# Four attention layers on one core: the second chunk's q moved to another buffer, under a new order of the steps

## The chip, the core and the metric

The kernel runs on one core of a Trainium2 chip. A core has five engines that each take their instructions strictly in the order in which they were issued: TensorE (PE in the profile, its weight loads PEld), VectorE (DVE), ScalarE (ACT), GpSimd (POOL) and SyncE (SP), which here issues nearly all DMAs. The engines wait for each other and for DMAs by semaphores. Operands lie in SBUF (128 partitions); TensorE writes to PSUM, which has eight banks here.

The metric is the time of one execution on the device in microseconds, as the median of several.

## What is computed

The input x has 2048 positions of 512 values. Four layers follow each other, A, B, A, B, each of the form x + attention(layernorm(x)), all in 32-bit floats. Both kinds have 32 heads of 16 values; they differ in what a position sees.

```python
# A: eight positions, two apart, backwards
idx = pos[:, None] - (arange(8) * 2)[None, :]
logits = einsum("bhsd,bhswd->bhsw", q, kg) * scale   # kg, vg: k, v gathered at idx
o = einsum("bhsw,bhswd->bhsd", softmax(logits), vg)
return o @ wo
# B: the last 256 positions
mask = (i - j >= 0) & (i - j < 256)
p = softmax(where(mask, q @ k.T * scale, -1e9))
return (p @ v) @ wo
x = x + A(layernorm(x)); x = x + B(layernorm(x)); x = x + A(layernorm(x)); x = x + B(layernorm(x))
```

## The kernel before

**Tiling.** The 2048 positions are cut into eight chunks of 256. The plan names the chunks of the first pair of layers A0 to A7 and B0 to B7 and those of the second pair A8 to A15 and B8 to B15. A chunk of B needs the chunk of A before it and k and v of its predecessor, so the chunks of the two layers run interleaved: A0, then B0 beside A1, B1 beside A2, and so on. Ahead of all stand "pA" and "pB", the loading and splitting of the weights.

**Precision.** Each float operand of a projection is split into a high and a low 16-bit part; a product is three matmuls, high by high, high by low and low by high. A projection step in the plan is such a triple: lines 1015 to 1017 for q, k and the transposed form, 1035 to 1038 for v and the output.

**A chunk of layer A** (`layer_a`, from line 1100). x is loaded (1088) and normalized (`norm`: means and squares on ScalarE, 936 and 939, a power on GpSimd, 942 to 948, the normalized tile `xn` on ScalarE, 964). Its high part is a copy (974), its low part a difference (970), and four transposing DMAs (976 and 977, on SP) bring both parts of both halves into `xh` and `xl`, with the features on the partitions. Chunk A0 and all chunks of B transpose on TensorE instead (986, 990, 995, 996). There are two buffers for `xn` and two for each of `xh` and `xl`. Then come sixteen steps each for q, k and v; ScalarE copies them out of PSUM (1131 for q, 1133 for k and v). Products of q with the shifted k (1152, sixteen tiles of 128x512 in four groups, on DVE or GpSimd) are summed over a head's values by TensorE (1160, one instruction group for each four tiles, so four sums). The softmax over eight logits is a chain on DVE (1183, 1186, the exponential on ScalarE 1212, 1189, 1192, 1195) with a high part (a copy on ScalarE, 1216) and a low part (1203, on DVE or GpSimd). TensorE spreads the weights over the heads' rows (1229), DVE multiplies by v (1242, eight times), GpSimd or DVE adds over the eight positions (1249 to 1251, or 1247), and `finish` splits the result (1059, 1061), projects it and adds it to x (1069).

**A chunk of layer B** (`layer_b`). After the projections, high and low parts of k and q (1273 on ScalarE, 1276 on DVE) go through DRAM (SP, 1286) into stacked operands `stk` (SP, 1297). A first pass of scores (1339, 1342) serves only the row maxima (DVE; 1352 in the first chunk of a layer, 1360 and 1356 later), which join the stack as two more rows through DRAM (1375 to 1399). A second pass (1432, 1434) gives scores less their maxima, ScalarE takes the exponential into a probability tile (1438), GpSimd masks it (1447), TensorE multiplies by v (1464), and ScalarE evicts (1500).

**Buffers that the change touches.** `po4` holds one q buffer (tag `q`) and one each for the outputs of A and B. `pp6` has three buffers of 6 KB a partition (tag `p6`): they stage the output weights of A and B at the start and hold B's probability tiles `p` later. For chunk A1 alone, k and v lie in buffers of another pool (`pos`) and its output in B's output buffer, so that A2 can use the `pkv` pair.

**What sets the order.** Each step is added to a plan with the engine it runs on, what it reads and writes, and a place number from a table written out in the file, `ORDER`, with one list for each chunk. An engine takes its steps by place. A negative number means that the step runs on its second choice of engine, at place -1 less the number; steps with two choices have an `alt`. A planner's model then merges the five queues into one order of issue and hands out the PSUM banks; it does not change the order within an engine. A list `W` places 110 triples of idle matmuls ("IDLE", line 1579), which compute nothing.

In the list of A2, entries 22 to 37 are the places of the q steps on TensorE, and after two for ScalarE's copies come the sixteen of the k steps. Entries 13, 14, 18 and 19 are its transposing DMAs on SP.

Of the kernel before, what the change touches and what calls it, by code (L numbers as in the profile page):

```python
# [11 lines left out]
F32 = mybir.dt.float32  # L12
# [6 lines left out]
P = 128  # L19
S = 2048  # L20
# [3 lines left out]
C = 256  # L24
NCH = S // C
W = 8
# [652 lines left out]
def kernel(  # L679
# [20 lines left out]
    def buf(name, shape, dtype, tag, label, cap=None, group=0):  # L700
        p, n = pools[name]
        return Buf(p, cap or n, shape, dtype, tag, label, group)
# [916 lines left out]
```

## Time and profile before

| | |
|---|---|
| median of three executions | 1426.83 us (1426.66 to 1429.48) |
| profiled execution | 1428.45 us, of which span 1426.7 us |
| mean granted TensorE clock | 0.957 |
| busy: PE, DVE, ACT, POOL | 1340.1, 1127.4, 817.5, 689.6 us |
| DMA | 130.46 MB, mean 91 GB/s |

The span runs from the first to the last instruction of the program. Busy time is what an engine spent on instructions, without waits. The granted clock is the share of full speed that the throttle gave TensorE. In the order in time of one engine, a line shows the start and the duration in us, the engine, the line of the kernel, the operation, what it writes and reads, how many are merged in it, and in brackets how long the engine stood idle before and what ended that. In a table of stages each engine has its busy time and, in brackets, its instructions. In a line of a group the numbers are the busy time in us, the mean of one in ns, and the idle time before them.

### The profile page before, as it was taken

The page shows a single profiled execution, that of the slowest core. Times are in us where ns is not written, and L with a number is a line of the kernel's source. Part 1 is how long each engine was busy: PE and PEld are TensorE (multiplying, and loading weights), DVE is VectorE, ACT ScalarE, POOL GpSimd, SP SyncE. Part 2 cuts the span into 40 slices and gives each one's busy share as a digit, 9 for nine tenths or more (in the row PEclk, how much of TensorE's full clock was granted, in tenths as well). Part 3 has the DMA queues.
Part 4 walks back from the last instruction along what each step waited for, and adds up shares of the span by engine and source line. Part 5 has one row for each costly group of instructions (what it writes and reads, how often), then busy time and mean ns, then how long its engine had stood idle before and what let it go on. Part 6 is the DMA issues. An engine that isn't in the chain of part 4 may idle for free.

```text
span 1426.7 us, 35354 instructions
## 1 busy us (share of the span) xinstructions
PE 1340.1 (94%) x13918; PEld 788.4 (55%) x13918; DVE 1127.4 (79%) x2095; ACT 817.5 (57%) x1296; POOL 689.6 (48%) x829
## 2 busy tenths in 40 slices
PE   9986989999899999989999898998999999999998
PEld 7741646546365564746556374654637456474654
DVE  6878696896978879697986859689696968869694
ACT  7732545565585556556565454656567555646664
POOL 4434353472835427362562716366273644727333
PEclk9986999999999999999999998999999999999999
DMA  8233242333242333424234143322333233242231
GB/s 248 78 72 85 73 100 71 93 85 99 70 122 68 72 100 97 114 54 116 66 97 122 45 115 90 111 69 72 107 86 114 69 91 88 82 118 65 79 100 54
DMA packets 135944, 130.46 MB, mean 91 GB/s; under 512 B 68448, under 2 KB 94560, under 8 KB 135776
## 3 DMA queue, kind: packets, MB, share of 16 engines
q1 hardware_dynamic: 135520, 127.93, 33.1%
q8 instruction: 109, 1.79, 0.5%
q14 instruction: 59, 0.48, 0.1%
q10 hardware_dynamic: 256, 0.26, 0.1%
HBM read 67.11 MB, written 43.48 MB: 78 GB/s over the span
## 4 chain that ended last, share of the span: by engine, by line
PE 64%; DVE 13%; POOL 7%; ACT 5%; issue 5%; DMA 4%; SPq 3%; ACTq 0%; POOLq 0%; DVEq 0%
PE banks L1015 10%; PE banks L1016 8%; PE banks L1017 8%; PE banks L1464 8%; PE banks L1037 4%; PE banks L1035 4%; PE banks L1432 4%; PE banks L1038 4%; PE banks L1160 4%; DVE pw L1242 3%; PE banks L1339 3%; DVE m L1356 3%; ACT p L1438 2%; POOL pw L1249 2%; PE banks L1342 2%
## 5 line engine op out<-in xcount | busy, mean ns | idle before, releaser
L1438 ACT ACTIVATE p<-banks,sclB 128x768 f32<-128x768 f32 x480 | 417.6, 899 | 241.5 <-PE banks L1434 194.8
L1447 POOL TENSOR_SCALAR_AFFINE_SELECT p<-p 128x1024 f32<-128x1024 f32 x240 | 262.4, 1101 | 334.6 <-ACT p L1438 325.2
L1356 DVE TENSOR_REDUCE m<-banks 128x2 f32<-128x512 f32 x448 | 297.6, 687 | 4.1
L1360 DVE COPY_PREDICATED banks<-maskt,banks 128x256 f32<-128x256 int16 x448 | 179.0, 424 | 80.8 <-PE banks L1342 79.6
L1464 PE MATMUL banks<-p,v 128*32 128x128 f32 (+1 forms) x3840 | 196.0, 332 | 5.3 <-POOL p L1447 4.3
L1152 DVE TENSOR_TENSOR pr<-kv,q 128x512 f32<-128x512 f32 x225 | 152.8, 731 | 37.2 <-PE banks L1160 21.5
L1464 PEld LDWEIGHTS banks<-p,v 128*32 128x32 f32 x3840 | 107.0, 110 | 97.8 <-issue 36.5
L1432 PE MATMUL banks<-stk,stk 64*128 64x256 f16 x960 | 133.9, 284 | 24.7 <-DVE m L1356 7.8
L1242 DVE TENSOR_TENSOR pw<-banks,kv 128x1024 f32<-128x1024 f32 x128 | 153.6, 1215 | 3.5 <-POOL o L1251 1.7
L1342 PE MATMUL banks<-stk,stk 48*128 48x128 f16 (+1 forms) x1024 | 130.8, 253 | 11.2 <-DVE m L1352 7.9
L1249 POOL TENSOR_TENSOR pw<-pw 128x512 f32<-128x512 f32 x100 | 127.2, 1272 | 12.8 <-DVE pw L1242 12.7
L1339 PE MATMUL banks<-stk,stk 48*128 48x128 f16 (+1 forms) x896 | 114.2, 254 | 19.4 <-DVE m L1356 6.5
L1432 PEld LDWEIGHTS <-stk 64*128 64x128 f16 x960 | 56.7, 95 | 109.9 <-issue 104.4
L1434 PE MATMUL banks<-stk,stk 64*128 64x128 f16 x960 | 108.4, 223 | 0.0
L1276 DVE SCALAR_TENSOR_TENSOR el<-banks,eh 128x512 f16<-128x512 f32 x64 | 42.6, 686 | 79.6 <-ACT eh L1273 52.6
L1339 PEld LDWEIGHTS <-stk 48*128 48x128 f16 x896 | 50.6, 95 | 99.0 <-issue 92.3
L1250 POOL TENSOR_TENSOR pw<-pw 128x256 f32<-128x256 f32 x100 | 72.7, 727 | 7.8
L1342 PEld LDWEIGHTS <-stk 48*128 48x128 f16 x1024 | 53.3, 97 | 33.7 <-issue 29.7
L1015 PE MATMUL banks<-xh,wA1h 128*128 128x256 f16 x256 | 70.9, 277 | 1.0 <-ACT wA1h L912 1.0
L1015 PE MATMUL banks<-xh,wB1h 128*128 128x256 f16 x256 | 71.2, 278 | 0.7 <-ACT xh L995 0.7
L1017 PE MATMUL banks<-xh,wA1l 128*128 128x256 f16 x256 | 70.8, 277 | 0.9 <-DVE wA1l L910 0.9
L1016 PE MATMUL banks<-xl,wB1h 128*128 128x256 f16 x256 | 70.9, 277 | 0.4 <-DVE xl L996 0.4
(201 smaller groups left out, 3117.9 us busy)
## 6 DMA issues: line engine op xcount, KB each, us to landing
stk<-re SPq DMA_DIRECT2D x256, 96.0 KB
re<-eh SPq DMA_DIRECT2D x128, 128.0 KB
xm<-y SPq DMA_DIRECT2D x32, 256.0 KB
re<-el SPq DMA_DIRECT2D x64, 128.0 KB
y<-xm SPq DMA_DIRECT2D x32, 256.0 KB
oc<-os SPq DMA_DIRECT2D x120, 64.0 KB
os<-scr SPq DMA_DIRECT2D x15, 512.0 KB
x<-in_A_x_dram SPq DMA_DIRECT2D x16, 256.0 KB
```

The lines of the kernel that those rows point to most:

```text
L1015: nc.tensor.matmul(ps[mp].t[:, i], wh, xh, start=k == 0, stop=False)
L1016: nc.tensor.matmul(ps[mp].t[:, i], wh, xl, start=False, stop=False)
L1017: nc.tensor.matmul(ps[mp].t[:, i], wl, xh, start=False, stop=k == 3)
L1242: nc.vector.tensor_mul(pw.t, pb.t.unsqueeze(1).broadcast_to([P, 2, W, 64]), v)
L1339: nc.tensor.matmul(ps.t[:, par, 0 : (2 - qb) * P], lhs, stk[hf, bef][r, col, qb * P :], start=True, stop=True)
L1342: nc.tensor.matmul(ps.t[:, par, (2 - qb) * P : 3 * P], lhs, stk[hf, now][r, col, : (1 + qb) * P], start=True, stop=True)
L1356: nc.vector.tensor_reduce(out=m.t[:, :, u, qb], in_=ps.t[:, :, 0 : 2 * P], op=ALU.max, axis=AX.X)
L1360: nc.vector.copy_predicated(t[:, :, 0:P], maskt[:, 0:P].bitcast(I16).unsqueeze(1).broadcast_to([P, 2, P]), t[:, :, 2 * P : 3 * P])
L1432: nc.tensor.matmul(o[:, two], k[:, jf * P : (jf + 1) * P], q, start=True, stop=True)
L1438: nc.scalar.activation(pt.t[:, :, 2 * i : 2 * i + 2].rearrange("p s m q -> p m s q"), ps.t[:, :, : 3 * P].rearrange("p m (s q) -> p m s q" ...
L1447: nc.gpsimd.affine_select(out=v, in_=v, pattern=[[0, 8], [-1 if b == 0 else 1, P]], compare_op=ALU.is_gt if b == 0 else ALU.is_ge, fill=0. ...
L1464: nc.tensor.matmul(o, v[:, jj, 17 * h : 17 * h + 32], rhs, start=z == 0 and (b == 0 or first), stop=z == 1 and b == 1, tile_position=(0, 3 ...
```

## The change

One line of `layer_a` takes the q tile of the second chunk of the first layer (A1) from a `pp6` buffer. The rest of the diff is the table `ORDER`: every list has new numbers. The numbers of steps and what each computes stay the same; some steps that two engines can do change engine. Below are the line, and of the table the list of A2 with the first entries of W (the others are cut).

```diff
@@ layer_a
         if l == 0 and c == 1:
 
-            q, o = buf("po4", [P, 4, C], F32, "q", f"q{l}_{c}"), buf("po4", [P, 4, C], F32, "ob", f"o{l}_{c}")
+            q, o = buf("pp6", [P, 4, C], F32, "p6", f"q{l}_{c}"), buf("po4", [P, 4, C], F32, "ob", f"o{l}_{c}")
             kv = {s: buf("pos", [P, 4, HALO + C], F32, "os", f"kv{l}_{c}_{s}") for s in (1, 2)}
@@ ORDER
-    "A2": [12, 8, 20, 22, 15, 19, 14, 15, 16, 31, 35, -35, 64, 31, 37, 40, -46, 62, 61, 35, 36, 312, 315, 318, 356,
-        357, 358, 359, 360, 364, 366, 367, 369, 370, 374, 376, 379, 117, 120, 296, 297, 298, 299, 300, 308, 309, 310,
-        365, 368, 371, 375, 380, 381, 382, 383, 100, 122, 390, 391, 392, 398, 399, 407, 408, 409, 393, 396, 400, 402,
...
+    "A2": [9, 8, 16, 22, 15, 20, 14, 15, 16, 31, 32, -46, 31, 30, 38, 39, 21, 29, 32, 36, 35, 310, 311, 312, 314,
+        315, 317, 323, 360, 373, 376, 378, 379, 380, 381, 384, 385, 119, 124, 199, 200, 201, 204, 242, 249, 258, 293,
+        361, 362, 365, 366, 370, 371, 372, 374, 93, 122, 382, 383, 397, 400, 405, 410, 414, 416, 390, 394, 395, 398,
...
```

Around A2's early k steps (places 199 to 201, 204, 242, 249 and 258 on TensorE) the new lists put these: 198 a logit sum of A1 (1160), 202 and 203 the transposes of B0 (990), 205 the second logit sum of A1, 206 to 221 B0's k, 222 to 240 B0's q with two steps of its v between, 241 and 250 the third and fourth sum of A1, the rest up to 257 B0's v, and 259 on the first scores of B0. Before, the order there was: 196 A1's first sum, 198 and 200 the transposes with idle triples around them, 201 to 216 B0's k, 217 to 232 its q, 233 A1's second sum, B0's v with the third sum in it, 251 A1's fourth sum, and 252 on the first scores.

On DVE, the new order around B0's first maxima is: A1's softmax (places 97 to 101), six of B0's maxima, a weighting of A1 (1242), two maxima, a weighting, the row transpose (1375). Before it was: two steps of the softmax and then its other three with maxima between them, up to nine maxima, the row transpose, and the first weighting.

831 rows, old and new, of the table ORDER are left out of this document.

## The prediction

> **What bounds the kernel now.** I read the page first, then the table of stages of 20 us, then the order in time of single engines at the stages that the table picks out. In what follows A0, A1, A2 and B0, B1 are chunks of the first layer A and the first layer B, as the plan names them.
>
> ```profile
> span 1426.7 us, 35354 instructions
> ...
> PE 1340.1 (94%) x13918; PEld 788.4 (55%) x13918; DVE 1127.4 (79%) x2095; ACT 817.5 (57%) x1296; POOL 689.6 (48%) x829
> ...
> PEclk9986999999999999999999998999999999999999
> ```
>
> The span is 1426.7 us and TensorE is busy for 1340.1 us of it, 94%. PEclk (a digit for each 35.7 us) has its low slices at 71 to 143 us (digits 8 and 6) and hardly any later. The table of stages (busy time of PE, weight loads, DVE, ACT, POOL, then the granted clock) shows why:
>
> ```profile
> 80.00:100.00 20.00, 14.58 (x89) 10.17 (x87) 13.72 (x18) 5.23 (x10) 5.09 (x5) 0.74 0.29 51
> ...
> 120.00:140.00 20.00, 11.53 (x53) 3.23 (x53) 18.09 (x52) 4.45 (x6) 14.01 (x18) 0.50 0.22 50
> ...
> 160.00:180.00 20.00, 20.00 (x204) 15.33 (x206) 11.96 (x34) 9.79 (x18) 7.21 (x6) 1.00 0.41 125
> ...
> 157.00:200.00 43.00, 42.69 (x447) 27.65 (x449) 33.62 (x79) 22.30 (x36) 15.29 (x17) 1.00 0.41 119
> ```
>
> From 80 to 157 us TensorE is not the bound: the clock falls to 0.74 in 80 to 100, and it is busy 11.53 of 20 us at a clock of 0.50 in 120 to 140, while DVE works 18.09 and POOL 14.01. There A1's attention and B0's first scores share DVE. From 157 us on TensorE is the bound (42.69 of 43 us at full clock), and so it stays. What the change wins before 157 us is kept only if TensorE then has less left to do, or gets there sooner.
>
> **The change, part by part.** (1) *The buffer.* A1's q moves from the one q buffer to one of the three that B's probabilities use. What it could free and what it could block:
>
> ```profile
> 108.87 2.50 DVE L1152 TENSOR_TENSOR pr<-kv,q 128x512 f32<-128x512 f32 x4 [1.26 <-PE banks L1160]
> 133.86 0.90 ACT L1438 ACTIVATE p<-banks,sclB 128x768 f32<-128x768 f32 x1
> 171.31 0.58 ACT L1131 COPY q<-banks 128x512 f32<-128x512 f32 x1 [1.04 <-PE banks L1017]
> ```
>
> The last products that read A1's q (L1152) end at 108.87 + 2.50 = 111.4 us; A2's q is written at 171.31. So the q buffer lies free for 60 us in the kernel before, and nothing waits for it. In the new order A2's first q step on TensorE has place 310 instead of 312, so it isn't used early there either. In its new place q is done at 111.4, and the first probabilities (L1438) come at 133.86: 22 us of slack hide that. Cost of the edit by itself: 0. Everything else is the order.
>
> (2) *A2's inputs and k earlier.* The four transposing DMAs of A2 move from SP places 31, 61, 62 and 64 to 29 to 32; they were issued here (first and second of four):
>
> ```profile
> 78.19 1.25 SPq L977 DMA_TRANSPOSE xl<-xn  x1
> 121.21 1.27 SPq L977 DMA_TRANSPOSE xl<-xn  x1
> ...
> 85.67 1.12 PE L990 MATMUL banks<-idf,xn 128*128 128x128 f32 x4 [3.81 <-ACT xn L986]
> 86.89 0.81 ACT L986 ACTIVATE xn<-y,rs 128x512 f32<-128x512 f32 x1 [1.27 <-PE banks L990]
> ...
> 90.65 0.42 PE L1015 MATMUL banks<-xh,wB1h 128*128 128x256 f16 x1
> 90.86 0.42 PE L1016 MATMUL banks<-xl,wB1h 128*128 128x256 f16 x1
> 95.06 0.27 PE L1015 MATMUL banks<-xh,wB1h 128*128 128x256 f16 x1
> 95.17 0.27 PE L1016 MATMUL banks<-xl,wB1h 128*128 128x256 f16 x1
> 110.83 1.66 PE L1160 MATMUL banks<-pr,sel 128*32 128x512 f32 x8 [0.35 <-DVE pr L1152]
> 157.75 0.27 PE L1015 MATMUL banks<-xh,wB1h 128*128 128x256 f16 x1
> ```
>
> In front of them on SP now stand only loads of B's weights; behind them comes A0's reload of x, wanted only at A0's end. Their old places on SP lie where that queue waits for B0's maxima, so their going gains nothing there. They free both xn buffers, of which A2 held one until the second of them: that is why B0's second normalization waited 1.27 us for the transpose of the first (L990). That wait goes. Seven of A2's sixteen k steps (three matmuls each, 0.11 us apart at full clock, 95.06 to 95.17) move from between A1's end and B1's transposes to places around B0's projections: three ahead of B0's transposes, one behind, three among B0's v. There TensorE was idle, 3.81 us ahead of 85.67 alone, so they cost nothing. Their old places are filled with A2's q steps: ahead of B1's first projection (157.75 us, where TensorE becomes the bound) stand seven of these instead of three. So four steps fewer are left behind that point: 4 x 3 x 0.11 = **1.3 us gained**.
>
> Against it: A1's second logit sum (L1160, 1.66 us at half clock) now stands between B0's transposes and B0's k, instead of behind B0's q. The 1.27 us won there pays for most of it; between 1.3 us sooner and 2.3 later (1.66 and one k step at half clock, 3 x 0.21, with no cover) for B0's stacks I take zero, since the k matmuls run at half clock there anyway (0.21 us apart at 90.65) and get the full one at 95.06 us whenever they begin.
>
> [...] The row: TensorE idles 3.81 us before 85.67 and the matmuls after it are 0.21 us apart. [...]
>
> (3) *A1's attention earlier against B0's first maxima.* A1's second group of products moves ahead of two of the weights' splits on DVE, so A1's last sums no longer queue behind it. Then DVE does A1's whole softmax before B0's first maximum, and A1's first weighting (L1242) after six of B0's maxima instead of after nine and the row transpose.
>
> ```profile
> 104.18 1.29 DVE L1276 SCALAR_TENSOR_TENSOR el<-banks,eh 128x512 f16<-128x512 f32 x2 [4.98 <-DMA re<-eh]
> ...
> 112.55 0.69 DVE L1183 TENSOR_REDUCE mx<-banks 128x64 f32<-128x512 f32 x1 [1.17 <-PE banks L1160]
> 113.27 0.69 DVE L1186 TENSOR_TENSOR e<-banks,mx 128x512 f32<-128x512 f32 x1
> ...
> 114.80 1.01 DVE L1189 TENSOR_REDUCE mx<-e 128x64 f32<-128x512 f32 x1
> ...
> 116.64 0.55 DVE L1192 RECIPROCAL mx<-mx 128x64 f32<-128x64 f32 x1
> ...
> 117.70 0.69 DVE L1195 TENSOR_TENSOR e<-e,mx 128x512 f32<-128x512 f32 x1
> ...
> 124.21 1.18 DVE L1242 TENSOR_TENSOR pw<-banks,kv 128x1024 f32<-128x1024 f32 x1
> ...
> 125.47 1.27 POOL L1249 TENSOR_TENSOR pw<-pw 128x512 f32<-128x512 f32 x1 [5.20 <-DVE pw L1242]
> 141.57 0.45 POOL L1251 TENSOR_TENSOR o<-pw 128x128 f32<-128x128 f32 x1
> ...
> L1352 DVE CUSTOM_DVE_ANT_0 unread<-banks,maskt 128x128 bf16<-128x128 f32 (+1 forms) x54 | 19.0, 353 | 7.9 <-ACT unread L939 1.8 <-ACT unread L936 0.8 <-PE banks L1342 0.5
> ...
> L1352 DVE DVE_READ_ACCUMULATOR2_ANT m<- 128x1 f32 x53 | 4.4, 83 | 0.0
> ```
>
> Before, DVE idled 4.98 us ahead of B0's last low parts and began A1's softmax at 112.55; its five steps are 0.69 + 0.69 + 1.01 + 0.55 + 0.69 = 3.6 us, and only the first two were done when B0's maxima came. The first weighting at 124.21 released POOL's sums at 125.47, and POOL then runs without a gap to 141.57 + 0.45 = 142.0. So A1's end is set by when POOL starts. In the new order it starts after the softmax (about 115 us by the rows: three products of 0.63 after 105.47, a logit sum, the five steps, the exponential between them) and six maxima of 0.87 (two of each row of L1352, 2 x (0.353 + 0.083)): 115 + 5.2 + 1.2 = 121.4 instead of 125.5, at best 4.1 us earlier. At worst DVE sets the end: the set of DVE steps up to A1's second residual is the same 40 in both orders, and what is done of it when B0's maxima come is only 3.6 - 1.4 - 1.0 = 1.2 us more (all five steps instead of two, less the first maximum, which lay ahead of 114.80); with B0's stacks 2.3 us late that is 1.1 us lost. Between 1.1 lost and 4.1 won I take **2.3 us gained**, on POOL's side of the middle, as POOL's rows are the ones without gaps.
>
> (4) *A0's end.* The low part of A0's weights goes from POOL to DVE, ahead of the scales of B's weights.
>
> ```profile
> 54.92 0.69 DVE L1195 TENSOR_TENSOR e<-e,mx 128x512 f32<-128x512 f32 x1
> 55.53 0.27 DVE L855 TENSOR_REDUCE a1B<-banks 4x1 f32<-4x128 f32 x1
> 56.61 0.90 DVE L863 TENSOR_TENSOR a1B<-a1B,idf 4x8 f32<-4x8 f32 x1
> 57.99 0.17 DVE L874 COPY pscB<-banks 128x8 f32<-128x8 f32 x1 [0.48 <-PE banks L1229]
> 58.50 2.36 DVE L1242 TENSOR_TENSOR pw<-banks,kv 128x1024 f32<-128x1024 f32 x2
> ...
> L1203 DVE TENSOR_TENSOR e<-e,eh 128x512 f16<-128x512 f32 x8 | 5.6, 694 | 0.8 <-ACT eh L1216 0.5
> ...
> 56.34 1.15 POOL L1203 TENSOR_TENSOR e<-e,eh 128x512 f16<-128x512 f32 x1 [2.96 <-ACT eh L1216]
> ```
>
> DVE would stand from 55.61 to 56.34 (ScalarE's copy must end first), do it in 0.69, and then the chain of small steps 55.53 to 57.51 (1.98 us): 59.0 us instead of 58.50 for the first weighting. **0.5 us lost** on a chain that leads through A0's end to B0. One product more ahead of A0's low part (0.63) lies beside TensorE's wait for the ScalarE copy; I take 0 of its bounds 0 to 0.63.
>
> (5) *The rest.* From A3 on, the order on TensorE is nearly the old one: most steps keep their place or move by a few. Of the steps that two engines can do, DVE hands seven products of layer A to POOL on balance (225 to 218), some 5 us of its 1127.4. I take 0, with bounds from the spread of equal stretches:
>
> ```profile
> 200.00:400.00 200.00, 188.02 (x1984) 106.50 (x1976) 161.67 (x275) 113.35 (x176) 112.42 (x132) 0.96 0.30 81
> 400.00:600.00 200.00, 193.33 (x2129) 118.67 (x2128) 159.34 (x278) 124.03 (x201) 91.86 (x112) 0.98 0.37 98
> ```
>
> Stretches with nearly the same work differ by 5.3 us in TensorE's busy time and by 0.02 in clock (0.02 x 200 = 4 us of full clock). A new order of the small steps, which moves the places where TensorE idles long enough for the clock to fall, can give or take about half of that in all: minus 3 to plus 6 us, more on the bad side, since any step late for TensorE costs both the wait and the clock.
>
> **Sum.** 1.3 + 2.3 - 0.5 + 0 = 3.1 us gained. The profiled execution took 1428.45 us (1426.7 of span and 1.75 around it), so 1425.35 by its own time; it stands 1.62 us above the median 1426.83 of the three runs shown, so **1423.7 us** as a median. The 3.1 us are just over 0.2% (2.85 us), which is about what a measurement of this kernel can tell from no change.
>
> **The rivals.**
> *Given back early (1427.1).* The buffer does nothing, as shown in (1), and the logit sum in front of B0's k makes B0's stacks 2.3 us late, so that (3) ends at its bad bound; with (2) and (4) that is -1.3 + 1.1 + 0.5 = 0.3. For it: B0's stacks are issued from B0's projections on, one after the other. Against it: the 1.27 us won there.
> *Slower by the later order (1429.7).* Place: the stages after 200 us in which TensorE waits for DVE, one in each chunk. Price: a stretch of half clock as long as that up to 95 us, some 10 us from the transposes on, costs half of it if it is full of matmuls, 5 us. From 6.0 us lost (a little more than one such stretch in 1200 us) it decides against the 3.1. For it: nearly every place number is new. Against it: the mean move is small.
> *The clock held (1421.6).* If A2's k steps keep the clock at 1.0 until 95 us, the 21 matmuls of B0's k from 90.65 to 95.06 save 21 x 0.10 = 2.1 us and B0's chain comes as much sooner: 1423.7 - 2.1. [...]
>
> **How the numbers follow.** Forecast 0.45 (1421.5 to 1426 by its own terms, 0.31 of it over the 0.2%), given back early 0.20 (0.18 within, 0.02 slower), slower by the later order 0.27, clock held 0.08. Over 0.2% faster: 0.31 + 0.08 = 0.39, and 0.01 for a later order that helps; within: 0.14 + 0.18 = 0.32 less that 0.01; slower: 0.29. Leaving out a tenth at each end, the range is 1419.5 (clock held and the good side of (5)) to 1431.5.
>
> **What would show it.** Right: four transposing DMAs of A2 before 65 us, k matmuls of A2 (L1015 to L1017 on wA1) ahead of 113 us, no wait of ScalarE for L990 at B0's second normalization, POOL's first sum of A1 some 2 to 4 us before 125.5, B1's k at about 155.5 instead of 157.75 us, and A2's q some 3 us before 171.31. Wrong: POOL's start unchanged, the gain at 200 us lost again by 1300, or a clock lower than 0.957 over the whole.

## The result, and the profile after

The changed kernel takes 1434.41 us (median of five executions, 1432.62 to 1436.40), the kernel before 1426.83 us beside it (1423.43 to 1429.48): the ratio is 1.0046 with a 95% interval of 1.0030 to 1.0062, so it is slower by 0.46%. (The ratios in this document are estimates over the executions of both kernels, and not the quotients of the two medians shown, which would be 1.0053 here.) The forecast was 1423.7 us in a range up to 1431.5; it was wrong. The profiled execution took 1432.99 us.

In the profile after, the lines of the kernel behind the table are one lower than before (L1352 is L1351, L1242 is L1241). The page of the kernel after:

```profile
span 1431.3 us, 35342 instructions
...
PE 1338.5 (94%) x13918; PEld 784.2 (55%) x13918; DVE 1122.7 (78%) x2091; ACT 817.7 (57%) x1292; POOL 700.8 (49%) x837
...
PEclk9996999999899999999999998999999999999999
```

In these two executions TensorE is busy for 1.6 us less than before (1338.5 against 1340.1), so what is lost in them is idle time of TensorE: 1431.3 - 1338.5 = 92.8 us against 1426.7 - 1340.1 = 86.6. The stages of the kernel after that answer to those shown of before (busy PE, weight loads, DVE, ACT, POOL, the granted clock, the DMAs' share and rate):

```profile
80.00:100.00 20.00, 14.83 (x108) 10.04 (x107) 15.34 (x21) 6.61 (x13) 7.33 (x11) 0.83 0.23 43
...
120.00:140.00 20.00, 12.55 (x53) 3.52 (x52) 18.41 (x47) 4.57 (x7) 15.65 (x19) 0.50 0.17 48
...
160.00:180.00 20.00, 19.10 (x183) 13.59 (x181) 10.65 (x31) 10.63 (x21) 9.91 (x11) 1.00 0.36 112
...
157.00:200.00 43.00, 41.54 (x396) 25.22 (x398) 30.33 (x70) 22.52 (x39) 17.99 (x20) 1.00 0.33 93
```

From 80 to 100 us the clock is now 0.83 instead of 0.74, and 108 matmuls run instead of 89. But from 157 to 200 us, where TensorE is the bound, it is busy for 41.54 us instead of 42.69. Single engines of the kernel after in order of time, at the places of the prediction's steps:

```profile
57.48 0.69 DVE L1202 TENSOR_TENSOR e<-e,eh 128x512 f16<-128x512 f32 x1 [0.68 <-ACT eh L1215]
58.63 1.22 SPq L976 DMA_TRANSPOSE xl<-xn  x1
59.64 1.21 DVE L1241 TENSOR_TENSOR pw<-banks,kv 128x1024 f32<-128x1024 f32 x1
81.56 0.28 PE L1014 MATMUL banks<-xh,wA1h 128*128 128x256 f16 x1
87.02 1.52 ACT L985 ACTIVATE xn<-y,rs 128x512 f32<-128x512 f32 x2 [4.17 <-POOL rs L947]
87.89 1.97 PE L989 MATMUL banks<-idf,xn 128*128 128x128 f32 x8 [5.17 <-ACT xn L985]
90.42 1.93 PE L1159 MATMUL banks<-pr,sel 128*32 128x512 f32 x8
92.29 0.39 PE L1014 MATMUL banks<-xh,wB1h 128*128 128x256 f16 x1
92.84 0.27 PE L1014 MATMUL banks<-xh,wB1h 128*128 128x256 f16 x1
92.95 0.27 PE L1015 MATMUL banks<-xl,wB1h 128*128 128x256 f16 x1
...
120.19 1.22 DVE L1241 TENSOR_TENSOR pw<-banks,kv 128x1024 f32<-128x1024 f32 x1
121.49 1.26 POOL L1248 TENSOR_TENSOR pw<-pw 128x512 f32<-128x512 f32 x1 [5.66 <-DVE pw L1241]
125.65 1.27 POOL L1248 TENSOR_TENSOR pw<-pw 128x512 f32<-128x512 f32 x1 [1.56 <-DVE pw L1241]
139.19 0.45 POOL L1250 TENSOR_TENSOR o<-pw 128x128 f32<-128x128 f32 x1
...
157.20 0.27 PE L1014 MATMUL banks<-xh,wB1h 128*128 128x256 f16 x1
170.65 0.60 ACT L1130 COPY q<-banks 128x512 f32<-128x512 f32 x1
```

Of the signs that the prediction named, the early ones are there: A2's last transposing DMA is issued at 58.63 us, its first k step stands at 81.56, ScalarE's two normalizations of B0 (L985) run as one piece with no wait for TensorE, and POOL's first sum of A1 comes at 121.49 instead of 125.47 us. Behind that less is left than was forecast: POOL ends 2.4 us sooner (139.19 + 0.45 against 142.02), B1's first projection comes 0.55 us sooner (157.20) where 2.3 were forecast, and A2's q 0.66 us (170.65) where 3 were. Not all of the rest is lost: by A2's q TensorE has also done twelve more matmuls than before (1072 against 1060, in rows further down), the four steps of step 2, which are 1.3 us of work. The old places of these steps are in the prediction.

### The profile page after: what moved, and what is told of

Read it like the earlier page. It is cut to its first block, busy times and chain, and to the rows that moved or that the text cites. A ratio compares the mean times of both kernels' runs of the same rounds, so it can differ in the third digit from the quotient of the medians.

```text
span 1431.3 us, 35342 instructions
## 1 busy us (share of the span) xinstructions
PE 1338.5 (94%) x13918; PEld 784.2 (55%) x13918; DVE 1122.7 (78%) x2091; ACT 817.7 (57%) x1292; POOL 700.8 (49%) x837
## 4 chain that ended last, share of the span: by engine, by line
PE 54%; DVE 13%; POOL 6%; issue 5%; ACT 4%; DMA 4%; SPq 2%; DVEq 0%; POOLq 0%; ACTq 0%
PE banks L1014 8%; PE banks L1463 7%; PE banks L1015 7%; PE banks L1016 7%; PE banks L1036 4%; PE banks L1034 4%; PE banks L1037 4%; PE banks L1431 4%; PE banks L1159 3%; DVE m L1355 3%; ACT p L1437 3%; DVE pw L1241 3%; PE banks L1338 3%; DVE banks L1359 3%; POOL pw L1248 2%
## 5 line engine op out<-in xcount | busy, mean ns | idle before, releaser
L1431 PE MATMUL banks<-stk,stk 64*128 64x256 f16 x960 | 136.1, 285 | 27.7 <-DVE m L1355 11.0
L1241 DVE TENSOR_TENSOR pw<-banks,kv 128x1024 f32<-128x1024 f32 x128 | 153.2, 1214 | 2.8 <-PE banks L1228 1.2
L1341 PE MATMUL banks<-stk,stk 48*128 48x128 f16 (+1 forms) x1024 | 129.5, 253 | 12.4 <-DVE m L1351 6.0
L1338 PE MATMUL banks<-stk,stk 48*128 48x128 f16 (+1 forms) x896 | 112.1, 254 | 17.3 <-DVE m L1355 9.2
L1431 PEld LDWEIGHTS <-stk 64*128 64x128 f16 x960 | 56.9, 95 | 114.5 <-issue 105.3
L1338 PEld LDWEIGHTS <-stk 48*128 48x128 f16 x896 | 50.3, 95 | 98.3 <-issue 93.3
L1151 POOL TENSOR_TENSOR pr<-kv,q 128x512 f32<-128x512 f32 x38 | 49.2, 1308 | 59.4 <-PE banks L1159 36.3
L1272 ACT ACTIVATE eh<-banks 128x512 f16<-128x512 f32 x64 | 37.2, 596 | 63.1 <-PE banks L1016 40.8
L1341 PEld LDWEIGHTS <-stk 48*128 48x128 f16 x1024 | 53.2, 96 | 32.0 <-issue 27.3
L1014 PE MATMUL banks<-xh,wA2h 128*128 128x256 f16 x256 | 70.5, 275 | 0.0
```

Of the source, the lines that this page charges most:

```text
L1014: nc.tensor.matmul(ps[mp].t[:, i], wh, xh, start=k == 0, stop=False)
L1151: E.tensor_mul(pr.t, window(kv[1].t, m, 64 * tq, 64)[:, 0], qb)
L1241: nc.vector.tensor_mul(pw.t, pb.t.unsqueeze(1).broadcast_to([P, 2, W, 64]), v)
L1338: nc.tensor.matmul(ps.t[:, par, 0 : (2 - qb) * P], lhs, stk[hf, bef][r, col, qb * P :], start=True, stop=True)
L1341: nc.tensor.matmul(ps.t[:, par, (2 - qb) * P : 3 * P], lhs, stk[hf, now][r, col, : (1 + qb) * P], start=True, stop=True)
L1431: nc.tensor.matmul(o[:, two], k[:, jf * P : (jf + 1) * P], q, start=True, stop=True)
```

## The experiments

Each kernel has runs of the kernel before beside it, whose medians lie between 1427.34 and 1428.41 us; the ratios below are against those. Most of the experiments are spliced orders: on each engine, all steps that the kernel before starts ahead of a seam stand in the one order, and all others behind them in the other order. "New until 170" is such a kernel: the new order for what starts ahead of 170 us, the old one for the rest. In the diffs, "-" is a piece of the table of the kernel that is named, "+" that of the experiment.

**1. The buffer alone.** The old order with A1's q in the other buffer, against the kernel before:

```diff
-            q, o = buf("po4", [P, 4, C], F32, "q", f"q{l}_{c}"), ...
+            q, o = buf("pp6", [P, 4, C], F32, "p6", f"q{l}_{c}"), ...
```

> The order of the kernel before, with the one line that puts A1's q in a probability buffer. All theories: the buffer itself costs and frees nothing, so 1426.8 us, within 3 us of the kernel before. If the edit itself is what costs (a buffer that B0's probabilities or the staged weights then miss), it stands at about 1434.

Measured: 1428.47 us, ratio 1.0005 (0.9994 to 1.0017). The buffer costs nothing and gives nothing.

**2. The order alone.** The kernel after with q left where it was:

```diff
-            q, o = buf("pp6", [P, 4, C], F32, "p6", f"q{l}_{c}"), ...
+            q, o = buf("po4", [P, 4, C], F32, "q", f"q{l}_{c}"), ...
```

> The new order with A1's q left in the q buffer. If the order alone makes the time, 1434.4 us within 3 us, as with the change. If the buffer makes it, 1427.

Measured: 1431.88 us, ratio 1.0036 (1.0022 to 1.0051). The order makes the loss.

**3. A seam at 227 us, both ways.** First the new order ahead and the old one behind, then the reverse (the pieces are of B1's list, against the kernel after and against the kernel before):

```diff
-    "B1": [... 613, 191, 107, 628, 198, 534, 255, 256, 553, ...
+    "B1": [... 612, 185, 105, 628, 191, 536, 253, 255, 554, ...
...
-    "B1": [... 612, 186, 101, 628, 192, 536, 256, 258, 554, ...
+    "B1": [... 613, 192, 104, 628, 199, 534, 257, 258, 553, ...
```

> The new order for all steps that the kernel before starts ahead of 227 us (through A2's end), the old order for the rest; the new buffer. Theory early (the start gives the loss away: A0 1.5 us late, and about 3 us lost by A2's end): 1433 to 1434 us. Theory late (the small moves of the later 1200 us cost it, each a little): 1427 us. Half and half: 1430.

> The reverse: the old order for all steps that the changed kernel starts ahead of 227 us, the new order for the rest. Theory early: 1427 us. Theory late: 1434 us. The two mixed kernels together tell whether the parts add up to the 7.6 us.

Measured: 1428.70 us for the new start alone, ratio 1.0009 (0.9998 to 1.0021); 1441.35 us for the new rest alone, ratio 1.0101 (1.0084 to 1.0118). The first says that the start neither gains nor loses by 227 us, as far as can be measured. The second is more than the whole loss of the change, and the trace of that kernel shows why it may not be read as the price of the late order (its lines are 19 higher than before):

```profile
226.08 9.63 SPq L1107 DMA_DIRECT2D x<-in_A_x_dram  x2
228.81 0.63 ACT L955 ACTIVATE unread<-x 128x512 bf16<-128x512 f32 x1 [4.46 <-DMA x<-in_A_x_dram]
231.68 1.15 POOL L1080 TENSOR_TENSOR ol<-oc,oh 128x512 f16<-128x512 f32 x1
232.89 0.61 PE L1054 MATMUL banks<-wB3h,ol 128*128 128x512 f16 x1 [5.30 <-POOL ol L1080]
```

At the seam a load of x stands on SP right ahead of the normalization that uses it. ScalarE waits 4.46 us for it (L955), a split of A2's output on POOL (L1080) stands behind that on POOL's queue, and TensorE waits 5.30 us for the split (L1054). The seam makes that wait; neither order has it.

**4. The late order, first try.** Seams at 339 us and around 1010 to 1258 us (pieces of B3's and B11's lists; the kernel before, the kernel after, the kernel before):

```diff
-    "B3": [... 889, 450, 454, 878, 438, 440, 887, 449, 451, ...
+    "B3": [... 893, 452, 454, 880, 439, 441, 888, 447, 449, ...
...
-    "B11": [... 2612, 1363, 1365, 2604, 1357, 1359, 2597, ...
+    "B11": [... 2611, 1365, 1367, 2602, 1357, 1359, 2597, ...
...
-    "B11": [... 2611, 1359, 1361, 2602, 1351, 1353, 2597, ...
+    "B11": [... 2612, 1357, 1359, 2604, 1351, 1353, 2597, ...
```

> Old order for every step that the kernel before starts ahead of 339 us, new order behind that (a seam where the two orders have nearly the same steps behind them, unlike that at 227 us). Theory 'one place': the loss of the new order sits between 1010 and 1258 us, where TensorE idles 3.4 us more in all three kernels that have the new order there; from 339 to 1010 us it idles 0.7 more and from 1258 us on 0.6 less, so this kernel takes 1427.3 + 3.5 = 1430.8 us. Theory 'spread': the 5.7 us between the kernel after and the one with the new start alone lie evenly over the 1200 us from 227 us on, so 1427.3 + 5.2 = 1432.5. Theory 'start': the late order costs nothing by itself, 1427.3.

> Old order, but for the steps from 1010 to 1258 us of the kernel before, which have the new one. Theory 'one place': 1427.3 + 3.4 = 1430.7 us, with the same waits of TensorE as in the kernel after (0.9 us for a maximum ahead of L1431 some 10 us into B11's scores, 1.1 us ahead of L1431 for the low part of exponentials, 1.05 us at B12). Theory 'spread': 248 of 1200 us, so 5.7 x 0.21 = 1.2 us, 1428.5. Theory 'start': 1427.3.

> The kernel after, but with the old order for the steps from 1010 to 1258 us. Theory 'one place': 3.4 us less than the kernel after, 1434.4 - 3.4 = 1431.0 us. Theory 'spread': 1.2 less, 1433.2. Theory 'start': 1434.4, no change.

> Old order, but for the steps from 339 to 1010 us of the kernel before, which have the new one. Theory 'one place': 0.7 us more idle of TensorE there, 1428.0. Theory 'spread': 671 of 1200 us, so 5.7 x 0.56 = 3.2 us, 1430.5. Theory 'start': 1427.3.

Measured, with ratios: old then new at 339 us 1443.33 (1.0106, 1.0086 to 1.0127); late part new 1440.56 (1.0084, 1.0066 to 1.0102); late part old 1434.96 (1.0046, 1.0028 to 1.0064); middle new 1445.83 (1.0123, 1.0103 to 1.0142). Three of the four lie above every number that the theories had, and "late part old" stands where the theory 'start' put it, which experiment 5 does not bear out. A seam at which the two orders differ by six steps costs more than all that was to be told apart. The traces show that the loss lies behind the seams: against the kernel before, "old then new at 339" is 1.2 us late when A4's q is written (at 337 us before), 12.1 at A6's (504) and 16.5 at A7's (593), but no later than that at A12's (1012, 14.0 us late); "late part new" is 4.6 us late at A15's q (1265) and 13.3 at the end, behind its second seam. A stage of the kernel before and of "old then new at 339":

```profile
480.00:500.00 20.00, 19.78 (x181) 14.04 (x181) 15.11 (x31) 10.07 (x17) 3.24 (x5) 1.00 0.16 45
```

```profile
480.00:500.00 20.00, 19.32 (x176) 9.61 (x177) 15.24 (x30) 11.39 (x21) 7.24 (x10) 0.80 0.28 78
```

A hundred and fifty us behind the seam the clock falls to 0.80 where it was 1.00, and DVE and TensorE do no more work than before (the kernel is some 12 us late there, so the work is not the same). As price lists these four runs are lost. What can be read in them is the same stage with and without a seam in it, and that was used to choose the next seams.

**5. Seams that are nearly none.** For every time the steps done by then were compared between the two orders. At 981 and 1248 us they differ by one step; at 148, 170 and 197 us by 8 to 15, mostly A2's early steps. The pieces are of the lists of A2, B1, B10 and B13, each against the kernel after:

```diff
@@ new until 148
-    "A2": [... 311, 312, 314, 315, 317, 323, ... 199, 200, 201, 204, 242, 249, 258, 293, ...
+    "A2": [... 315, 318, 356, 357, 358, 359, ... 199, 200, 201, 204, 242, 308, 309, 310, ...
@@ new until 170
+    "A2": [... 311, 312, 314, 315, 358, 359, ... 199, 200, 201, 204, 242, 249, 258, 293, ...
@@ new until 197
-    "B1": [... 355, 118, 155, 117, 156, 80, 82, 81, 83, ...
+    "B1": [... 355, 116, 155, 115, 156, 79, 81, 80, 82, ...
@@ new until 981
-    "B10": [... 2540, 820, 440, 2577, 829, 2460, 1288, ...
+    "B10": [... 2542, 819, 438, 2576, 829, 2450, 1286, ...
@@ new until 1248
-    "B13": [... 3201, 1037, 563, 3231, 1048, 3123, 1637, ...
+    "B13": [... 3202, 1035, 560, 3231, 1047, 3128, 1639, ...
```

> New order (and new buffer) for every step that the kernel before starts ahead of 148 us, old order behind that; at 148 us the two orders differ by eight steps, all of them ahead in the new one. Theory 'gained, then given back': in the four profiles with the new start, POOL's first sum of A1 is 4.8 us earlier than in the six with the old one, B1's first projection 1.4 us, with 1.4 us more of TensorE's work done; it is given back from 171 to 227 us, where TensorE idles 1.9 us more in the new order. With the old order from 148 us on the idle stays at the old 0.25 us (171 to 197) and 3.5 us (197 to 225), the gain is kept, and the kernel takes 1427.7 - 1.4 = 1426.3 us. Theory 'nothing gained': DVE and POOL set A1's end anyway, A2's y comes at 224.5 us as before, 1427.7. Theory 'seams cost': like the four spliced kernels so far, 1433 or more, with new waits of TensorE of over 3 us in the 150 us behind the seam.

> The same with the seam at 170 us, where TensorE has done four more steps of A2's q and k. Theory 'gained, then given back': both parts of the gain are kept, 1.4 us sooner and 1.4 us more work done, 1427.7 - 2.8 = 1424.9 us. Theory 'nothing gained': 1427.7. Theory 'seams cost': 1433 or more.

> New order for every step that the kernel before starts ahead of 197 us, old order behind. With the seam at 170 us the kernel took 1425.0 us, with the seam at 227 us 1428.7. TensorE idles 1.0 us more in the new order from 171 to 197 us and 1.0 us more from 197 to 227 us. Theory 'half each': 1425.0 + 1.0 to 1.9 = 1426.0 to 1426.9 us. Theory 'all of it behind 197 us': 1425.0. Theory 'all of it ahead of 197 us': 1428.7.

> The kernel after, with the old order for every step that the kernel before starts from 981 us on; at the seam the two orders differ by one step. Theory 'late place': the 4.1 us that TensorE idles more between 1012 and 1226 us go, and the 0.5 to 1 us that the new order gains behind 1258 us go too, 1434.4 - 3.4 = 1431.0 us. Theory 'spread': (1426.8 - 981) of 1200 us of 5.7, so 2.1 less, 1432.3, with the idle growing as in the kernel after. Theory 'seams cost': 1436 or more, with a jump of over 2 us of idle in the 50 us behind the seam.

> The kernel after, with the old order for every step that the kernel before starts from 1248 us on, where the orders differ by one step. Theory 'late place' (the loss lies between 981 and 1248 us, where TensorE idles 4.1 us more): 1434.4 us or 0.5 to 1 more, since the new order's end idles less. Theory 'the end': the loss lies behind 1248 us, 1427.4 as with the seam at 981 us.

| new order until | median, us | ratio to before | 95% interval |
|---|---|---|---|
| 148 us | 1430.88 | 1.0018 | 1.0006 to 1.0030 |
| 170 us | 1425.04 | 0.9984 | 0.9972 to 0.9997 |
| 197 us | 1428.32 | 1.0005 | 0.9991 to 1.0018 |
| 227 us | 1428.70 | 1.0009 | 0.9998 to 1.0021 |
| 981 us | 1427.40 | 1.0002 | 0.9989 to 1.0014 |
| 1248 us | 1433.08 | 1.0035 | 1.0023 to 1.0047 |
| the end (the kernel after) | 1434.41 | 1.0046 | 1.0030 to 1.0062 |

This table is the answer to where the time went. With the new order until 170 us and the old one behind it the kernel is 0.16% faster than before, so the early part of the change does win time: about 2.5 us (1427.55 - 1425.04), with an interval that is only just clear of nothing. Its trace keeps the lead over the kernel before: 3.2 us at A2's q, 4.6 at A15's (1265 us). With the new order until 197 us nothing of it is left that can be measured. From there to 981 us the new order costs nothing that can be measured. Between 981 and 1248 us it loses 5.7 us by the medians (1433.08 - 1427.40) and 4.7 by the ratios (0.0033 x 1428), since the kernel before stood at 1427.60 beside the one and at 1428.41 beside the other. The end may add 1.3, which the intervals don't tell from nothing.

The seam at 148 us doesn't fit: there TensorE waits for B0's maxima, which DVE takes in the old order again. The first of its waits from 138 to 162 us (engine, what it waited for, us in total, times, longest) is this; the same wait takes 0.9 us with the seam at 170 us and 1.5 in the kernel before:

```profile
PE banks L1363 <- DVE m L1373: 2.8, 4, 1.4
```

**6. The late order behind other starts.** The old order until 981 us and the new one behind it; then the new one until 170, the old one until 981 and the new one again (pieces of B10's list, against the kernel before; they are the same in both):

```diff
-    "B10": [... 2542, 825, 439, 2576, 835, 2450, 1279, 1282, ...
+    "B10": [... 2540, 826, 441, 2577, 835, 2460, 1281, 1282, ...
```

> The kernel before, with the new order (and the new buffer) from 981 us on. Theory 'late place': 1427.6 + 3.4 = 1431.0 us, with 3.4 to 4.1 us more idle of TensorE between 1012 and 1226 us. Theory 'spread': 1427.6 + 2.1 = 1429.7. Theory 'seams cost': 1434 or more.

> New order ahead of 170 us, old order from 170 to 981 us, new order from 981 us on. Theory 'each part by itself': 1425.0 + 0.65 = 1425.7 us (up to 1429 by the interval of that part). Theory 'the late order costs 7 us behind the new start': 1425.0 + 7 = 1432.0. Theory 'the late order costs 7 us behind the new middle only': 1425.7, like the first.

Measured: 1428.25 us, ratio 1.0012 (0.9998 to 1.0026), and 1428.54 us, ratio 0.9999 (0.9984 to 1.0015). The first is 0.0012 over before, the second 0.0015 over "new until 170" (0.9984). So behind the old order of the middle the late order costs some 2 us (0.0012 x 1428 = 1.7, 0.0015 x 1428 = 2.1), with intervals that reach from nothing to about 5, and behind the new order of the middle 4.7 by the same reckoning, with an interval of some 2 to 7. Whether the middle makes a difference to it is not settled by these times; the new start alone does not.

TensorE's idle time agrees. The same stretch of 228 us in four kernels, of which the first and the third have the old order there, the second and the fourth the new one (before, after, new until 981, old until 981); idle is 228 less the busy time:

```profile
1012.00:1240.00 228.00, 219.21 (x2380) 123.04 (x2377) 192.59 (x328) 136.21 (x215) 123.98 (x147) 0.98 0.33 89
```

```profile
1012.00:1240.00 228.00, 215.03 (x2343) 121.82 (x2345) 186.22 (x316) 134.30 (x210) 127.38 (x147) 0.98 0.32 89
```

```profile
1012.00:1240.00 228.00, 218.25 (x2385) 123.24 (x2383) 191.71 (x327) 135.78 (x215) 124.03 (x147) 0.99 0.32 89
```

```profile
1012.00:1240.00 228.00, 216.80 (x2343) 122.21 (x2341) 188.06 (x319) 136.19 (x214) 125.78 (x149) 0.98 0.32 89
```

With the old order TensorE idles 8.8 and 9.8 us, with the new one 13.0 and 11.2. The other traces agree, leaving out the four kernels of experiment 4 and the new rest alone, which their seams spoil: in all seven with the old order it idles 8.4 to 9.8 us, in all seven with the new one 11.2 to 13.0, of which the two behind the old middle have the least (11.2 and 12.0). DVE, too, does less in the same time (186.2 and 188.1 us of work against 192.6 and 191.7), and POOL a little more. TensorE's waits in that region, before and after:

```profile
PE banks L1432 <- ACT p L1438: 1.8, 4, 0.7
PE banks L1339 <- DVE m L1356: 1.8, 4, 0.7
PE banks L1432 <- DVE m L1356: 1.2, 3, 0.7
```

```profile
PE banks L1431 <- DVE m L1355: 2.9, 8, 0.9
PE banks L1431 <- ACT p L1437: 2.9, 4, 1.1
PE banks L1338 <- DVE m L1355: 2.2, 5, 0.9
PE banks L1431 <- DVE el L1275: 1.1, 1, 1.1
```

The scores of B wait for banks that DVE's maxima and ScalarE's exponentials still read: the second pass (L1431) 2.9 us for maxima instead of 1.2 and 2.9 for exponentials instead of 1.8, the first pass (L1338) 2.2 for maxima instead of 1.8, and once there are 1.1 us for a low part.

**7. Two of these waits attacked.** In the kernel after, one maximum of B11 moved ahead of the second of two weightings of A12 on DVE, and one weighting of A13 behind the next two steps of B12, of which the second is a maximum:

```diff
-    "A12": [... 1355, 453, 2606, 1361, 454, 1360, ...     "B11": [... 2603, 1358, 1362, 1374, ...
+    "A12": [... 1355, 453, 2606, 1362, 454, 1360, ...     "B11": [... 2603, 1358, 1361, 1374, ...
-    "A13": [... 1472, 499, 2823, 1482, ...                "B12": [... 963, 2825, 1480, 1484, 2839, ...
+    "A13": [... 1472, 499, 2823, 1484, ...                "B12": [... 963, 2825, 1480, 1483, 2839, ...
```

> The kernel after with two steps of DVE moved: in B11 a row maximum ahead of A12's second of two successive weightings, in B12 a weighting of A13 behind the next maximum. Theory 'local waits': the waits of TensorE that these steps end (0.90 us at 1059.3 and 0.92 to 1.05 us at 1142 to 1144) go, 1.5 to 1.9 us less idle between 1010 and 1258 us, 1434.4 - 1.7 = 1432.7 us. Theory 'DVE as a whole': DVE's work in these stages is the same, so the waits only move to the next steps, less than 0.5 us of idle goes, 1434.4.

Measured: 1433.82 us, ratio 1.0045 (1.0029 to 1.0061). The place in B11, first in the kernel after, then in this one (whose lines are 20 higher than in the kernel after):

```profile
1056.29 2.35 DVE L1241 TENSOR_TENSOR pw<-banks,kv 128x1024 f32<-128x1024 f32 x2
1059.30 0.29 PE L1431 MATMUL banks<-stk,stk 64*128 64x256 f16 x2 [0.90 <-DVE m L1355]
```

```profile
1056.51 0.70 DVE L1375 TENSOR_REDUCE m<-banks 128x2 f32<-128x512 f32 x1
1058.39 0.29 PE L1358 MATMUL banks<-stk,stk 48*128 48x256 f16 x2 [0.61 <-ACT p L1457]
```

The wait of 0.90 us behind the two weightings is gone, and the next scores wait 0.61 us for ScalarE instead. In B12 the wait of 0.92 us (1142.21 in the kernel after) stands unchanged at 1141.07, and that of 1.05 us has become one of 0.79 for a maximum. From 1012 to 1240 us TensorE idles 0.5 us less (12.5 instead of 13.0). That is what the theory "DVE as a whole" said: most of the waits only move. Which of the many steps moved in these chunks makes the loss is not settled.

**8. The low part of A0's weights back on POOL** (against the kernel after):

```diff
-    "A0": [... 49, 51, 52, 52, 53, 138, 55, ...
+    "A0": [... 49, 51, 52, 52, -22, 138, 54, ...
```

> The kernel after with the low part of A0's weights back on POOL (part 4 of the change undone). Theory 'part 4 costs 0.5 us': A0's first weighting 0.5 us sooner than in the kernel after (59.6 us there, 58.5 before), A0's second residual and B0's first projection sooner by as much. Theory 'covered': A0's second residual stays at 81.2 us, since what sets it is another step. The whole stays within 1.5 us of 1434.

Measured: 1434.95 us in one execution. Its first weighting of A0 and A0's second residual (lines 20 higher than in the kernel after), and that residual in the kernel after:

```profile
58.37 1.22 DVE L1261 TENSOR_TENSOR pw<-banks,kv 128x1024 f32<-128x1024 f32 x1 [0.52 <-PE banks L1248]
80.33 0.74 DVE L1088 SCALAR_TENSOR_TENSOR y<-banks,sclA,y 128x512 f32<-128x512 f32 x1
```

```profile
80.45 0.73 DVE L1068 SCALAR_TENSOR_TENSOR y<-banks,sclA,y 128x512 f32<-128x512 f32 x1
```

The weighting is 1.27 us sooner than in the kernel after (59.64), the residual 0.12 us (80.45 to 80.33). "Covered" is right: part 4 costs next to nothing at A0's end.

## Why the prediction was wrong

*Step 1, the buffer at 0:* right (experiment 1).

*Steps 2 and 3, 1.3 and 2.3 us gained:* the size was right and did not last. With the old order behind 170 us the early part wins 2.5 us (0.4 to 4.0), where steps 2 to 4 came to 3.1. The mechanism was in part another than the one the steps gave, so that the nearness of the two numbers is partly luck. The first 170 us, up to A2's q, in the kernel before, after, and "new until 170":

```profile
0.00:171.31 171.31, 145.65 (x1060) 94.39 (x1062) 124.94 (x278) 88.87 (x157) 70.38 (x106) 0.87 0.40 109
```

```profile
0.00:170.65 170.65, 144.14 (x1072) 93.60 (x1073) 123.81 (x276) 89.78 (x160) 69.95 (x109) 0.90 0.40 112
```

```profile
0.00:168.15 168.15, 141.28 (x1060) 92.14 (x1062) 124.53 (x277) 88.59 (x157) 69.77 (x106) 0.90 0.40 110
```

Before and "new until 170" have done 1060 matmuls by then, the one at 171.31 us, the other at 168.15. TensorE's idle time has not shrunk, it is 1.2 us more (168.15 - 141.28 against 171.31 - 145.65); its busy time is 4.4 us less, at a mean clock of 0.90 instead of 0.87. Step 2 said that the k steps run in idle time and cost nothing; in truth idle time arose elsewhere (5.17 us ahead of L989 instead of 3.81) and the time at half clock became shorter. So the rival "the clock held" was nearer to how the gain is made. The prediction had half clock end at 95.06 us as before, whenever B0's k begins; it lasted from 87.89 to about 92.8 us instead of from 85.67 to 95.06: the matmuls of B0's k stand 0.11 us apart already at 92.84 us. In place of most of B0's k, the transposes, one k step of A2 and the logit sum (1.93 us) ran at half clock. That made up for the later start of B0's k, whose ninth step begins at 95.06 us before and at 95.14 after. What brought the clock back sooner is not shown. That the earlier return belongs to the order, and not to one execution, is shown by the clock that the other traces recorded. Counted from its begin, which lies in the hole, this stretch of half clock lasts 10.24 us in the kernel before (84.75 to 94.99) and 6.83 us in the kernel after (85.95 to 92.78). Tables of 10 or 20 us give 10.2 us for "the buffer alone" and for the new rest alone, both with the old order there, and 6.8 for "the order alone" and the new order until 170 and until 227 us. Counted over all nineteen traces it is 10.2 us in six of the seven with the old order there (6.8 in the seventh), and 6.8 in eleven of the twelve with the new one (3.4 in the twelfth). The next stretch, which no step of the prediction weighed, became shorter too: 27.31 us in the kernel before (115.47 to 142.78) and 23.89 us in the kernel after (116.65 to 140.54). Over the nineteen traces it is 27.3 us in all seven, 23.9 in eleven of the twelve (20.5 in the other).

In step 3 POOL's start was right (121.4 us forecast, 121.49 measured), but POOL then waits 1.56 us for the second weighting (125.65), which stands behind two more maxima on DVE. The premise that POOL's rows have no gaps fell; that its end came 2.4 us sooner, close to the 2.3 of the sum, is the start's 4.0 less this wait.

*Step 4, 0.5 us lost:* the first weighting was late by more (59.64 against 58.50, as the row of 57.48 shows), but it is covered (experiment 8). The term was 0.

*The rival "given back early"* was right on the outcome of the start, but not on the place. B0's stacks were not late by 2.3 us (the last loads of them are issued at 120.70 us instead of 119.98); the gain is lost behind A2's q. From A2's q to B0's last probabilities and on to A2's end, in the kernel before, after and "new until 170":

```profile
171.31:196.60 25.29, 25.03 (x262) 14.48 (x260) 23.43 (x49) 11.57 (x18) 7.75 (x9) 1.00 0.47 130
196.60:224.23 27.63, 24.09 (x217) 10.12 (x220) 26.12 (x42) 12.59 (x21) 25.84 (x30) 0.81 0.30 65
```

```profile
170.65:197.82 27.17, 25.71 (x253) 13.41 (x250) 23.69 (x49) 12.14 (x19) 12.67 (x14) 1.00 0.34 97
197.82:227.35 29.53, 24.98 (x225) 10.27 (x227) 27.82 (x44) 12.28 (x20) 26.04 (x31) 0.83 0.35 72
```

```profile
168.15:193.67 25.52, 25.11 (x262) 14.50 (x260) 23.84 (x51) 11.66 (x18) 7.29 (x9) 1.00 0.44 132
193.67:220.67 27.00, 23.21 (x217) 9.73 (x220) 25.62 (x42) 12.59 (x22) 25.77 (x30) 0.87 0.30 66
```

The first stretch takes 25.29, 27.17 and 25.52 us, with 0.3, 1.5 and 0.4 us of idle TensorE; the second 27.63, 29.53 and 27.00. Together the kernel after takes 3.8 us longer for them than the kernel before (56.70 against 52.92), and with the old order in them "new until 170" takes 0.4 us less. With the table of seams, which puts the loss between 170 and 197 us, this agrees in size but not in place, since half of it lies in the second stretch. "New until 197" has a seam of its own there: in its trace a lead over the kernel before of 2.3 us at A2's q is 1.0 at A3's (253 us), and at A4's (337) it is 1.2 us late, so that much of its loss may come behind the seam, in the old order (two traces of one order, the kernel before and "the buffer alone", stray by up to 3 us on the way, so this is no proof). Which steps lose these 3 us stays open. And it was not so that TensorE is the bound from 157 us on, as the prediction has it: in the second stretch it idles 3.5 of 27.63 us in the kernel before and has a clock of 0.81. In the first stretch of the kernel after, TensorE waits for B1's stacks and for A2's q:

```profile
PE banks L1338 <- DMA stk<-re: 0.6, 2, 0.3
PE banks L1463 <- ACT q L1130: 0.4, 1, 0.4
```

*Step 5, the rest at 0:* this is the step that failed. The prediction bounded it by -3 to +6 us and took zero; measured from "new until 170" it loses 8.9 us by the ratios (1.0046 - 0.9984 = 0.0062) and 9.4 by the medians (1434.41 - 1425.04). By the ratios 3.0 of them come with the seam moved from 170 to 197 us, nothing more up to 981, and 4.7 between 981 and 1248 us. The first part lies in A2 and B1, ahead of the chunk A3 with which the words of step 5 begin: no step priced that stretch. In the second TensorE idles 11.2 to 13.0 us of 228 instead of 8.4 to 9.8, in waits for DVE's maxima and ScalarE's exponentials. The rival "slower by the later order" had the right kind of cause (TensorE waits for DVE) and was given 0.27; its price, 1429.7 us, was too small. The reason against it, a small mean move of the places, was none: at 339 us the two orders differ by six steps, and joining them there cost 15 us.

How much of the late loss is wait and how much clock can be estimated from the traces. From 1012 to 1240 us TensorE idles 3.5 us more in the five traces that have the new order from the start through this stretch (12.6 us on average) than in the seven with the old one there (9.1). Its half clock in that stretch lasts 11.3 us on average in the seven traces with the new order and 8.9 in the seven with the old one (10.24 us in each of the two traces of the kernels before and after); if that time is full of matmuls, half of the difference is lost, 1.2 us. Together that is 4.7 us, and with so few traces the exactness of it is chance; but by this estimate most of the loss is wait. Step 5 had any late step cost both the wait and the clock; from 1050 to 1070 us of the kernel after TensorE idles 3.34 us in all, the wait of 0.90 us among it, at a clock of 1.00.

## What to carry to other kernels

An order written out by a search is one piece: a change of it is not priced by the steps that are easy to name, and "the rest is nearly the old one" is no reason for a zero. Price each stage where TensorE is close to the bound by its waits, and where no row prices them, widen the range instead. To find what an order loses, splice old and new at a time where the sets of finished steps differ by one step, look at the seam's own waits first, and move the seam. The number of differing steps does not tell a seam's cost by itself: with six of them (339 us) it was 15 us, with 8 to 15 (170 us) none that shows. Moving the seam found here the one part that wins, 1425.04 us with the new order until 170 us, which is faster than both kernels.

## What was not expected of the hardware

The stretches of half clock have few lengths. In all nineteen traces the granted clock is either 0.5 or 1. Its stretches of half clock last 3.41, 6.83, 10.24 and 27.31 us in the trace of the kernel before and 3.41, 6.83, 10.24 and 23.89 us in that of the kernel after; in none of the nineteen is there another length than 1, 2, 3, 6, 7 or 8 times 3.41 us, but for the stretch that the end of the program cuts short. Between these two traces the one at the hole became shorter by 3.41 us and the next one by 3.42, which by estimate is up to 1.7 us of work each (half of 3.41, if it is full of matmuls). Runs of one and the same kernel differ in clock too, and in one kernel most of the scatter goes with it: of the twelve runs of "old until 981" the eight at a mean clock of 0.958 to 0.962 took 1424.2 to 1428.9 us, and the four at 0.954 to 0.957 took 1432.0 to 1433.1. In others it does not: "new until 1248" took 1429.8 us at 0.961 and 1436.1 at 0.960. And a wait of 5 us on a chain of SP, ScalarE and POOL was made by the mere place of one load in SP's queue (226.08 us in experiment 3): the queue is as much a part of an order as TensorE's.
